# Four transformer layers on one core: another row of the planner's cost table, more of the MLP's blocks evacuated by VectorE, and a new order list

## The chip, the cores and the metric

The kernel runs on one core of a Trainium2 chip. The metric is the device time of one execution in microseconds (us). Three runs of the kernel before gave 449.42, 451.48 and 449.11 us, so the median is 449.42 us.

The core has five engines, each with its own instruction stream. TensorE (PE) multiplies matrices into PSUM, a memory of eight banks of 128 x 512 f32. PE's records come in two rows, PEld for the loading of the 128-row stationary operand and PE for the matmul itself. ScalarE (ACT) computes Exp and GELU. VectorE (DVE) and GpSimd (POOL) do the elementwise work, and only DVE and ACT read PSUM here. SyncE (SP) issues most of the DMAs.

## The reference

One sequence of 2048 tokens with 512 features goes through attention, MLP, attention, MLP, each behind a layernorm without gain and added to the residual. Both attention layers share one set of weights, and both MLP layers another.

```python
def _A_ref(x, wqkv, wo):                      # D = 512, H = 32 heads of 16, W = 256
    qkv = (x @ wqkv).reshape(B, S, 3, H, Dh).transpose(2, 0, 3, 1, 4)
    q, k, v = qkv[0], qkv[1], qkv[2]
    scores = einsum("bhqd,bhkd->bhqk", q, k) * Dh ** -0.5
    mask = (i - j >= 0) & (i - j < W)         # each query sees itself and 255 keys before it
    p = softmax(where(mask, scores, -1e9))
    return einsum("bhqk,bhkd->bhqd", p, v).transpose(...).reshape(B, S, D) @ wo

def _B_ref(x, w1, b1, w2, b2):                # F = 1792
    return gelu(x @ w1 + b1, approximate=True) @ w2 + b2

x = x + A(layernorm(x)); x = x + B(layernorm(x))
x = x + A(layernorm(x)); x = x + B(layernorm(x))
```

## The kernel before, in words

**Tiles.** The 2048 tokens are 16 tiles of 128; the two passes over the layers make 32 tiles in a row (`NT`), and two tiles make a block of attention, so there are 16 blocks (`NB`). All weights stay on the core, as does the residual `X`.

**Attention of a block.** Q and K (the Q group at `lnq`, the K group at `kv`) and V are projected from the transposed, normalised tile `xnTA`. The scores come in *visits* of 512 columns (function `visit`). A visit is 16 or 24 short matmuls on a quarter of the array's rows each, four of them side by side, and takes four PSUM banks. Two Exps on ACT (L948), each 128 x 1024, take the visit to `E`. There are 152 visits and 304 Exps. A mask (L969, on DVE or POOL) clears the triangles. Then `pv` multiplies `E` with `Va` in two *halves* of 64 matmuls, each of 17 columns of the array, for every pair of chunks of heads; DVE transposes the result (L1034), divides by the sums (L1037, L1039) and transposes again (L1044); `outproj` multiplies with `Wo`.

**MLP.** The 32 tiles are ten jobs (`JOBS`): two of 2 tiles, six of 4 tiles, two of 2 tiles. A job has 14 blocks of 128 hidden features (`FC`), each of four matmuls over 256 or 512 columns. GELU is taken in one of two ways. For the first `NPRE(J)` blocks DVE adds the bias and copies from PSUM to `gT` (L1103), and ACT then takes GELU of two blocks at once inside `gT` (L1106). For the other blocks ACT reads PSUM itself, with the bias (L1114). The last two jobs, which start when attention has ended, use only the second way. Then 14 matmuls of 512 columns per tile multiply with `W2`, and DVE adds to `X` (L790).

**What sets the order.** All operations are nodes with an engine, a duration and dependencies (`_List.add`). A list of node numbers written out by hand, `ORDER`, sets the order on every engine: each engine does its nodes in the order of the list. `TURNS` says, for each node that two engines could do (masks, PSUM evacuations of Q and V, the division), which one does it. `BANKS` gives the PSUM banks of each group. `_List.run` walks the list with a table of costs to get planned starts, which `_Sched.spread` uses to place some of PE's waits; the order itself comes from `ORDER`. Semaphore waits are worked out from the reads and writes.

**PE's code in the cost table.** One row of the table, `CODE`, says how the planner sees PE's instruction stream: an edge after 194 instructions and then after every 256, 2.009 instructions for each matmul, and a time after each edge before which PE may not go past the next one. In `_List.run`:

```python
                while edge < till:
                    at = nd["start"] + late + nd["dur"] * (edge - code) / (till - code)
                    late += max(0.0, loaded - at)
                    loaded = max(at, loaded) + self.CODE[3]
                    edge += self.CODE[1]
```

The program on PE has 8764 matmuls, each with its load of the stationary operand, and some 80 instructions that only wait: 69 pieces of 256 instructions.

Of the kernel before, what the change touches and what calls it, by code (L numbers as in the profile page):

```python
# [185 lines left out]
class _List:  # L186
# [5 lines left out]
    CODE = (194.0, 256.0, 2.0090, 3700.0)  # L192
# [38 lines left out]
    def run(self):  # L231
# [11 lines left out]
        last_lock = None  # L243
        code, edge, loaded = 2.0, self.CODE[0], 0.0
        last_geo, last_tab = None, "exp"
# [53 lines left out]
def bass_interleave_layers__sliding_block__dense_activation_gelu__prompt_kernel(  # L299
# [60 lines left out]
    def NPRE(J):  # L360
        return 10 if J < 2 else 6
# [13 lines left out]
    with ExitStack() as kctx:  # L375
        S_ = _Sched(nc, kctx)

        def sb(name, shape, dtype=dt.bfloat16):
# [832 lines left out]
```

## Time and profile before

| | |
|---|---|
| median of three runs | 449.42 us (449.11 to 451.48) |
| the profiled execution's own time | 449.14 us |
| its span, first to last instruction | 447.4 us |
| granted TensorE clock | 1.000 |
| PE busy | 425.2 us, 95% |
| PEld busy | 232.2 us, 52% |
| DVE busy | 373.5 us, 83% |
| ACT busy | 386.4 us, 86% |
| POOL busy | 239.9 us, 54% |

The profiled execution ran 449.14 us, 1.74 us of which lie outside the span. A busy PE in this table is not a PE at its peak, because a matmul's record covers the array's latency also, and the records of successive matmuls overlap: for the pace the reader should take the starts of successive matmuls. PEld rows are the more exact ones for where PE stood still, because each matmul has one load just ahead of it. "issue" as the releaser of a wait means that no semaphore event of the profile ended it.

### The profile page before, as it was taken

Reading aid. Unit: us, or ns where it says so; the run is one execution under the profiler, and the core shown is the slowest. Engines: PE = TensorE matmul, PEld = TensorE weight load, DVE = VectorE, ACT = ScalarE, POOL = GpSimd, SP = SyncE. Lnnn points to the kernel's source line nnn. Section 1 sums busy time; section 2 is a strip of 40 time slices with the busy share of each in tenths; the row PEclk is TensorE's granted clock in tenths of the full one; section 3 lists DMA queues with packets and bytes.
Section 4 is the critical chain, followed back from the end, with each engine's and each line's share of the span. In section 5 each row is a group of like instructions: output and inputs, shape, how many; then the busy total and the mean of one; then the engine's idle time right before and its main releaser. Section 6 shows DMA issues by size and latency. Waiting matters only on the chain.

```text
span 447.4 us, 19245 instructions
## 1 busy us (share of the span) xinstructions
PE 425.2 (95%) x8691; PEld 232.2 (52%) x8764; DVE 373.5 (83%) x745; ACT 386.4 (86%) x458; POOL 239.9 (54%) x301
## 2 busy tenths in 40 slices
PE   8999999888999999999999999999999999999997
PEld 5555655645544545545445445445454454545665
DVE  6999989899998989888999898998898876775512
ACT  2999999999999998899997999889979999892452
POOL 4764786755865357643356457672455454444330
DMA  9920000001120112010220101301031003002021
GB/s 264 370 88 4 4 1 3 5 3 50 43 56 13 50 51 75 25 37 16 68 67 3 39 24 50 74 15 49 27 85 50 15 5 94 22 8 62 0 84 48
DMA packets 39903, 22.88 MB, mean 51 GB/s; under 512 B 24460, under 2 KB 39308, under 8 KB 39820
## 3 DMA queue, kind: packets, MB, share of 16 engines
q1 hardware_dynamic: 39404, 21.24, 16.4%
q8 instruction: 69, 1.13, 1.0%
q10 hardware_dynamic: 416, 0.39, 0.3%
q14 instruction: 14, 0.11, 0.1%
HBM read 13.77 MB, written 7.86 MB: 48 GB/s over the span
## 4 chain that ended last, share of the span: by engine, by line
PE 70%; ACT 15%; DVE 10%; issue 2%; DMA 2%; POOL 0%
PE ps L32 69%; ACT E L948 10%; ACT gT L1114 2%; ACT gT L1106 2%; DVE TT L1034 2%; DVE E L969 1%; DMA xnTB<-scr_x 1%; DVE stat L734 1%; DVE QT L720 1%; ACT L948 1%; DVE X L790 1%; DVE xs_ L753 1%; DMA scr_x<-xs_ 1%; DVE Va L720 1%; DVE OT L1044 1%
## 5 line engine op out<-in xcount | busy, mean ns | idle before, releaser
L948 ACT ACTIVATE E<-ps 128x1024 bf16<-128x1024 f32 x304 | 285.7, 1044 | 23.9 <-PE ps L32 23.0
L969 POOL TENSOR_TENSOR E<-E,mask 128x512 bf16<-128x512 bf16 (+1 forms) x130 | 134.8, 1052 | 89.9 <-DVE E L969 40.8
L32 PE MATMUL ps<-xnTB,W_sb 128*128 128x512 bf16 (+1 forms) x560 | 115.2, 337 | 1.4 <-issue 0.3
L32 PE MATMUL ps<-W_sb,gT 128*128 128x512 bf16 (+1 forms) x421 | 108.4, 373 | 4.3 <-issue 3.0
L32 PE MATMUL ps<-xnTA,Wqkv_sb 128*128 128x256 bf16 (+1 forms) x544 | 74.6, 267 | 1.5 <-ACT E L948 0.7
L32 PEld LDWEIGHTS ps<-xnTB,W_sb 128*128 128x128 bf16 x560 | 51.6, 98 | 42.9 <-ACT E L948 3.8
L32 PE MATMUL ps<-QT,KT 32*64 32x320 bf16 (+4 forms) x2976 | 65.5, 258 | 4.0 <-ACT E L948 2.0
L790 DVE TENSOR_TENSOR X<-X,ps 128x512 bf16<-128x512 bf16 x63 | 42.4, 676 | 25.3 <-PE ps L32 25.0
L32 PEld LDWEIGHTS ps<-W_sb,gT 128*128 128x128 bf16 x462 | 41.5, 98 | 42.2 <-issue 6.7
L1114 ACT ACTIVATE gT<-ps,b1T 128x512 bf16<-128x512 f32 (+1 forms) x84 | 45.7, 598 | 20.1 <-PE ps L32 19.8
L32 PEld LDWEIGHTS ps<-xnTA,Wqkv_sb 128*128 128x128 bf16 x544 | 47.0, 98 | 24.2 <-ACT E L948 3.5
L32 PEld LDWEIGHTS ps<-QT,KT 32*64 32x64 bf16 x2976 | 27.6, 103 | 51.0 <-ACT E L948 32.5
L969 DVE TENSOR_TENSOR E<-E,mask 128x512 bf16<-128x512 bf16 (+1 forms) x132 | 49.1, 402 | 3.0 <-ACT E L948 3.0
L741 POOL TENSOR_TENSOR statmv<-statmv,mhalf 128x1 f32<-128x1 f32 x64 | 36.6, 575 | 22.8 <-DVE statmv L738 18.9
L32 PE MATMUL ps<-E,Va 64*17 64x128 bf16 (+3 forms) x3872 | 46.0, 229 | 2.5 <-ACT E L948 0.9
L1034 DVE STREAM_TRANSPOSE TT<-ps 128x1024 f32<-128x1024 f32 x32 | 39.8, 1244 | 9.4 <-PE ps L32 9.1
L32 PEld LDWEIGHTS ps<-E,Va 64*17 64x17 bf16 x3872 | 36.7, 85 | 19.5 <-PE ps L32 8.0
L1039 POOL TENSOR_TENSOR TM<-TT,Rc 128x512 bf16<-128x512 f32 x22 | 23.3, 1058 | 44.0 <-DVE E L969 17.8
L734 DVE BATCH_NORM_STATS2 stat<-X 128x6 f32<-128x512 bf16 x64 | 43.0, 678 | 2.7 <-DMA X<-in_A_x_dram 2.4
L1078 POOL TENSOR_TENSOR X<-X,b2b 128x512 bf16<-128x512 bf16 x32 | 36.7, 1157 | 13.2 <-DVE E L969 5.7
L1103 DVE TENSOR_SCALAR gT<-ps,b1T 128x512 bf16<-128x512 f32 (+1 forms) x56 | 35.5, 643 | 8.0 <-PE ps L32 7.7
L864 DVE TENSOR_TENSOR KT<-ps,parmask 128x1024 bf16<-128x1024 f32 x30 | 36.2, 1210 | 2.7 <-PE ps L32 2.5
(56 smaller groups left out, 348.5 us busy)
## 6 DMA issues: line engine op xcount, KB each, us to landing
scr_x<-xs_ SPq DMA_DIRECT2D x44, 128.0 KB, 1.9
W_sb<-in_B_w_dram SPq DMA_DIRECT2D x2, 1792.0 KB, 15.4
xnTB<-scr_x SPq DMA_DIRECT2D x26, 128.0 KB, 2.7
xnTA<-scr_x SPq DMA_DIRECT2D x18, 128.0 KB, 2.7
out_dram<-X SPq DMA_DIRECT2D x15, 128.0 KB, 1.8
Wqkv_sb<-in_A_wqkv_dram SPq DMA_DIRECT2D x4, 256.0 KB, 4.9
X<-in_A_x_dram SPq DMA_DIRECT2D x1, 1024.0 KB, 9.2
Wqkv_sb<-in_A_wqkv_dram SPq DMA_DIRECT2D x1, 512.0 KB, 6.4
```

Of the source, the lines that this page charges most:

```text
L32: return self.e.matmul(*a, **k)
L734: add("dve", lambda e, B: e.bn_stats(stat6[:, k6, :], X[:, t, :]), 590, reads=["X%d" % t], writes=["st%d" % k6], prio=prio)
L741: add("pool", lambda e, B: e.tensor_tensor(out=statmv[:, k, 1:2], in0=statmv[:, k, 1:2], in1=mhalf[:], op=ALU.pow), 535, reads=["ve%d" % k ...
L790: add("dve", lambda e, B: e.tensor_tensor(out=X[:, t, :], in0=X[:, t, :], in1=ps[:, B[g][0], :], op=ALU.add), d_psum(512), reads=["X%d" % ...
L864: add("dve", lambda e, B, g=g, i=i: e.tensor_tensor(out=KT[:, kb, :, 2 * i : 2 * i + 2, :].rearrange("p a c q -> p a (c q)"), in0=ps[:, B[ ...
L948: add("act", lambda e, B, g_=g_, gi=gi: e.activation(E[:, 2 * gi : 2 * gi + 2, e0 : e0 + 512], ps[:, B[g_][0] : B[g_][0] + 2, :], AF.Exp, ...
L969: op = lambda e, B, Ew=Ew, Mw=Mw: e.tensor_tensor(out=Ew, in0=Ew, in1=Mw, op=ALU.mult)
L1034: add("dve", lambda e, B: e.transpose(TT[:, s].rearrange("p a c q d -> p a (c q d)"), ps[:, B[g][0] : B[g][0] + 2, :].rearrange("p a n -> ...
L1039: mul = lambda e, B: e.tensor_tensor(out=TM[:, sm].rearrange("p c q a d -> p a (c q) d"), in0=TT[:, s, :, :, :, 0:Dh].rearrange("p a c q d ...
L1078: add("pool", lambda e, B: e.tensor_tensor(out=X[:, t, :], in0=X[:, t, :], in1=b2b[:], op=ALU.add), 1110, reads=["X%d" % t, "b2b"], writes ...
L1103: add("dve", lambda e, B, g=g, fc=fc: e.tensor_scalar(out=gT[:, fc, 0:M], in0=ps[:, B[g][0], 0:M], scalar1=b1T[:, fc : fc + 1], scalar2=No ...
L1114: add("act", lambda e, B, g=g, fc=fc: e.activation(gT[:, fc, 0:M], ps[:, B[g][0], 0:M], AF.Gelu_apprx_tanh, bias=b1T[:, fc : fc + 1], scal ...
```

## The change

Three things are edited. The fourth number of `CODE` goes from 3700 to 3000 (ns). `NPRE` goes from 10 and 6 to 12 and 8, so that in the first two jobs 12 of 14 blocks, and in the next six 8 of 14, are evacuated by VectorE ahead of a GELU inside SBUF. `ORDER`, `TURNS` and `BANKS` are replaced as a whole. The number in `CODE` puts no instruction into the program; it enters the planned starts, which decide where some of PE's waits are placed.

```diff
-    CODE = (194.0, 256.0, 2.0090, 3700.0)
+    CODE = (194.0, 256.0, 2.0090, 3000.0)
...
     def NPRE(J):
-        return 10 if J < 2 else 6
+        return 12 if J < 2 else 8
...
         ORDER = [
-            18, 21, 22, 23, 24, 25, 26, 27, 28, 29, 15, 16, 4, 5, 0, 8, 9, 10, 3, 17, 1, 2, 14, 35, 19, 36, 37, 38,
...
+            3222, 3228, 3229, 3230, 3231, 3232, 3233, 3234, 3235, 3236, 3237, 3238,
         ]
         TURNS = [
-            1, 1, 0, 1, 1, 1, 1, 1, 0, 0, 0, 0, 1, 0, 1, 0, 1, 0, 1, 0, 0, 0, 0, 0, 1, 1, 1, 0, 1, 1, 0, 0, 1, 1, 1,
...
+            1, 1, 0, 1, 1, 0, 0, 1, 0, 1, 0, 0, 1, 1, 1, 0, 1, 0, 1, 0, 0, 0, 0, 0, 1, 1, 0, 1, 1, 0, 1, 1, 1, 1, 0,
...
         BANKS = (
-            "2 6 0 7 5 4 2 6 3 1 6 5 0 1267 3467 5 2 0134 7 6 4523 1 2367 0 5 3412 0 7 5 1267 0 6734 5 2 0134 67 "
...
+            "2 6 1 0 7 3 5 6 2 0 6 7 1234 0 5634 7 2 0134 7 6 4523 6 4501 7 2 3 0167 3 5 6745 1 2367 0 1 4523 67 "
```

Counted in the two programs, these instructions change their number; everything else, PE's 8764 matmuls, the 304 Exps, the 18 table loads of ACT and all DMAs included, is there as often as before, in another order:

| engine, operation, output | before | after |
|---|---|---|
| DVE bias and copy to `gT`, 128x512 / 128x256 | 36 / 20 | 48 / 24 |
| ACT GELU from PSUM, 128x512 / 128x256 | 48 / 36 | 36 / 32 |
| ACT GELU inside `gT`, 128x1024 / 128x512 | 18 / 10 | 24 / 12 |
| evacuation of V, 128x512: DVE / ACT | 25 / 7 | 18 / 14 |
| evacuation of Q, 128x512: DVE / ACT | 29 / 5 | 28 / 6 |
| evacuation of Q, 128x256: DVE / ACT | 0 / 4 | 2 / 2 |
| evacuation of `xnTA`: DVE / ACT | 12 / 2 | 11 / 3 |
| evacuation of `xnTB`: DVE / ACT | 4 / 2 | 5 / 1 |
| mask 128x512: DVE / POOL | 116 / 102 | 111 / 107 |
| division of the attention output: DVE / POOL | 10 / 22 | 8 / 24 |
| epsilon of the layernorm: DVE / POOL | 29 / 35 | 25 / 39 |

414 rows, old and new, of tables (BANKS, ORDER, TURNS) are left out of this document.

## The prediction

> **What bounds the kernel now.** I read the page first (busy shares, the chain), then three stretches, then who waits on PE's side.
>
> ```profile
> span 447.4 us, 19245 instructions
> PE 425.2 (95%) x8691; PEld 232.2 (52%) x8764; DVE 373.5 (83%) x745; ACT 386.4 (86%) x458; POOL 239.9 (54%) x301
> PE 70%; ACT 15%; DVE 10%; issue 2%; DMA 2%; POOL 0%
> ```
> ```profile
> core 0: us, PE busy (x) PEld busy (x) DVE busy (x) ACT busy (x) POOL busy (x), PEclk, DMA share, GB/s
> 20.00:120.00 100.00, 91.03 (x2318) 54.30 (x2330) 92.88 (x198) 97.75 (x115) 67.72 (x76) 1.00 0.09 27
> 120.00:400.00 280.00, 272.26 (x5653) 139.37 (x5700) 245.98 (x471) 258.11 (x291) 146.56 (x175) 1.00 0.16 42
> 400.00:447.40 47.40, 44.10 (x520) 27.92 (x522) 18.96 (x39) 19.13 (x39) 14.37 (x19) 1.00 0.15 46
> ```
>
> Two stages have two bounds. From 20 to 120 us ACT is busy 97.75 of 100 us: Exp sets the pace. From 120 to 400 PE is busy 272.26 of 280 while ACT and DVE have 22 and 34 us to spare, and after 400 PE runs alone. A microsecond that PE stands still between 120 and 447 is lost unless another of its waits shrinks for it. Over PE's waits from 120 to 400 (total us, times, longest):
>
> ```profile
> PEld ps L32 <- ACT E L948: 32.0, 89, 0.6
> PEld ps L32 <- issue: 16.3, 72, 0.4
> ...
> PEld ps L32 <- ACT gT L1114: 2.1, 6, 0.5
> PEld ps L32 <- DVE gT L1103: 1.9, 5, 0.4
> ...
> PEld ps L32 <- DMA xnTB<-scr_x: 0.8, 1, 0.8
> ```
>
> Most of this passes while the matmul before still runs, but the list says whom PE meets: Exp, 89 times.
>
> **Code edges, the part the change speaks of.** PE's code comes in by DMA, in 69 packets, so 16 KB or some 254 instructions each (twice 8764 over 69). The row below is the page's; the next two rows are the DMA rates of 79 to 83 us in slices of 0.1 us, where no other transfer runs, and of 27 to 29 us in slices of 0.05; then PE's loads around two stands.
>
> ```profile
> q8 instruction: 69, 1.13, 1.0%
> ```
> ```profile
> GB/s 0 0 164 0 0 0 0 0 0 0 0 0 0 0 0 0 0 0 0 0 0 0 0 0 0 0 0 0 0 0 0 0 0 0 0 0 0 164 0 0
> ```
> ```profile
> GB/s 0 0 0 0 0 0 0 0 0 0 0 0 0 0 0 0 0 0 0 0 0 0 0 0 0 0 0 0 0 0 0 0 0 328 0 0 0 0 0 0
> ```
> ```profile
> 26.83 0.15 PEld L32 LDWEIGHTS ps<-QT,KT 32*64 32x64 bf16 x15 [0.21 <-DVE QT L720]
> 27.57 0.10 PEld L32 LDWEIGHTS ps<-QT,KT 32*64 32x64 bf16 x1 [0.58 <-issue]
> ```
> ```profile
> 80.92 0.40 PEld L32 LDWEIGHTS ps<-E,Va 64*17 64x17 bf16 x29
> 81.68 0.12 PEld L32 LDWEIGHTS ps<-E,Va 64*17 64x17 bf16 x11 [0.36 <-issue]
> ```
> ```profile
> 0.00:27.56 27.56, 24.87 (x344) 14.88 (x348) 23.24 (x52) 18.98 (x24) 17.05 (x40) 1.00 0.91 292
> 0.00:81.67 81.67, 74.21 (x1610) 43.76 (x1619) 73.36 (x163) 71.83 (x86) 53.00 (x81) 1.00 0.31 101
> ```
>
> PE stands in the middle of a visit for 0.58 us and in the middle of a PV half for 0.36, and no semaphore ends it. Where: 348 loads lie ahead of the first, 1619 ahead of the second; with as many matmuls and the program's 7 and 25 wait instructions that is 703 and 3263, and both are 191 more than a multiple of 256. So these are code edges. A packet starts at 79.2 to 79.3, PE goes over the edge at 81.68, 2.4 us later; the next packet starts at 82.7 to 82.8, 1.1 us after the crossing, as at the other place (27.57, packet at 28.65). So PE seems unable to cross two edges less than 2.4 + 1.1 = 3.5 us apart. I count with 3.55.
>
> **The price of the new edges.** I add up PE's own pace between successive edges (instructions 192 + 256k) in both programs' orders. The pace, from starts of successive instructions:
>
> ```profile
> 413.36 2.75 PE L32 MATMUL ps<-W_sb,gT 128*128 128x512 bf16 x12 [0.16 <-issue]
> 416.82 1.91 PE L32 MATMUL ps<-xnTB,W_sb 128*128 128x256 bf16 x16
> ```
> ```profile
> 207.40 0.21 PEld L32 LDWEIGHTS ps<-QT,KT 32*64 32x64 bf16 x24 [0.42 <-ACT E L948]
> 207.76 0.10 PEld L32 LDWEIGHTS ps<-W_sb,gT 128*128 128x128 bf16 x1
> ```
> ```profile
> 412.45 0.61 PEld L32 LDWEIGHTS ps<-E,Va 64*17 64x17 bf16 x64 [0.42 <-PE ps L32]
> 413.12 2.49 PEld L32 LDWEIGHTS ps<-W_sb,gT 128*128 128x128 bf16 x13
> ...
> 413.32 1.25 DVE L1034 STREAM_TRANSPOSE TT<-ps 128x1024 f32<-128x1024 f32 x1 [0.32 <-PE ps L32]
> ```
>
> A 512-column matmul takes (2.75-0.38)/11 = 0.216 us, a 256-column one 0.109, a visit 0.36, a PV half 0.67 (0.38 and 0.27 being single records). One block as an example, the 30th: before it holds 1.03 PV halves, 1.84 visits, 4 long and 12 short matmuls, 3.5 us; after it holds 1.5 halves, one visit, 1 long and 6 short ones, 2.2 us.
>
> In PE's stage, 120 us on, before has six blocks under 3.55 us (3.33, 3.10, 3.39, 3.45, 3.53, 3.54), 1.0 us short together. The new order has eleven (3.32, 3.10, 2.99, 2.84, 2.18, 3.23, 3.37, 3.11, 3.50, 3.44, 2.54), 5.4 us short. In ACT's stage there are six before (5.1 us short) and five after (3.30, 2.29, 2.43, 1.78, 2.12; 5.8 us short).
>
> What is paid of the 5.4: waits inside a block lengthen it. PE met Exp for 32.0 of 280 us, 0.34 us per 3 us block; taken off each short, at most all of it, leaves 2.5. If the close blocks hold no waits it is 5.4. I take 3.6, nearer 2.5, because each stand also lets ACT and DVE run ahead and a later wait shrinks. Before pays a part of its 1.0 too: at the edge in the row below 0.27 us are idle where some 0.12 lie between two such loads (0.216 less the load's 0.10), so 0.15; over the six I take 0.35.
>
> ```profile
> 172.05 0.53 PEld L32 LDWEIGHTS ps<-W_sb,gT 128*128 128x128 bf16 x3 [0.27 <-issue]
> ```
>
> So **+3.2 us**, between +2.1 and +5.1 if the floor of 3.5 holds.
>
> [...]
>
> **Semaphore waits in the new order.** For every wait of PE on ACT, DVE or POOL I take PE's pace between the matmul that feeds the other engine and the waiting one, and set against it the durations on the path (Exp below) with 0.34 us for two hops, an estimate from the 0.26 us between the end of the PV loads (413.06) and the transpose (413.32). Where the pace is shorter, PE comes too early. Those shortfalls sum to 27.2 us before and 24.8 after; beyond the first 100 us of PE's work, 6.2 and 5.7. In PE's stage that is **-0.4**. In ACT's stage PE's earliness costs nothing as long as ACT runs on: I take 0 there, with -2.0 (the rest of the difference) and +2.0 (edges starving ACT) as ends.
>
> **VectorE ahead of GELU, and the moved evacuations.** By form:
>
> ```profile
> L948 ACT ACTIVATE E<-ps 128x1024 bf16<-128x1024 f32 x304 | 285.7, 1044 | 23.9 <-PE ps L32 23.0
> ...
> L1114 ACT ACTIVATE gT<-ps,b1T 128x512 bf16<-128x512 f32 x48 | 30.0, 692 | 1.7 <-PE ps L32 1.7
> ...
> L1103 DVE TENSOR_SCALAR gT<-ps,b1T 128x512 bf16<-128x512 f32 x36 | 26.6, 740 | 6.7 <-PE ps L32 6.4
> ...
> L1106 ACT ACTIVATE gT<-gT 128x1024 bf16<-128x1024 bf16 x18 | 18.7, 1056 | 0.0
> ...
> L720 DVE CAST Va<-ps 128x512 bf16<-128x512 f32 x25 | 16.9, 680 | 1.8 <-PE ps L32 1.7
> ...
> L1114 ACT ACTIVATE gT<-ps,b1T 128x256 bf16<-128x256 f32 x36 | 15.7, 472 | 18.4 <-PE ps L32 18.1
> ...
> L1103 DVE TENSOR_SCALAR gT<-ps,b1T 128x256 bf16<-128x256 f32 x20 | 9.0, 469 | 1.4 <-PE ps L32 1.3
> ...
> L1106 ACT ACTIVATE gT<-gT 128x512 bf16<-128x512 bf16 x10 | 6.0, 626 | 0.0
> L722 ACT ACTIVATE Va<-ps 128x512 bf16<-128x512 f32 x7 | 4.3, 611 | 0.0
> ```
>
> ACT loses 12 x 692 + 4 x 472 = 10.2 us and gains 6 x 1056 + 2 x 626 = 7.6; seven evacuations of V come to it, 7 x 611 = 4.3; the other moves cancel to -0.2. ACT: +1.5 us. DVE gains 12 x 740 + 4 x 469 = 10.8, loses 7 x 680 = 4.8 and some 4 of masks and small operations: +2.0. POOL has half its time idle. In PE's stage ACT's 22 and DVE's 34 spare us cover this; without that cover ACT's share would add 1.1. In ACT's stage nothing covers it: ACT's work ahead of the 57th visit (some 120 us) grows by 0.4 by the same sums: **+0.4**. PSUM banks come free sooner when DVE takes a block: at most the 2.1 us of PE's waits on L1114; but 1.9 us of waits on L1103 stand beside it and grow with the count (72 against 56). I take 0.
>
> **SP and the table.** Each of the 44 round trips through DRAM, all in other places of SP's queue, has the same two DMAs; one late arrival was met by PE, 0.8 us, so -0.8 to +0.8, taken 0. The 18 table loads of ACT stay.
>
> **The sum.** +3.2 - 0.4 + 0.4 = +3.2 us on a span of 447.4: 450.6, and with the 1.74 us outside the span 452.3 us. The profiled execution (449.14) lies 0.28 below the median of 449.42; against the median it is +0.6%.
>
> **The rivals.** *The stands are hidden anyway* (no change): PE pauses at an edge, ACT and DVE catch up, and the next wait on Exp is shorter. For it: 32.0 us of such waits, 89 of them. Against it: the largest shorts (1.37, 1.01, 0.71 us) are longer than any wait there (0.6). It gives some +1, 450 us. *The edges are free below 3.5 us* (faster): the two stands were something else, a block that is asked for sooner comes sooner, and the new order keeps its better waits: -2.4 of shortfalls, -0.35 of stands, 446.4 us. It decides if PE goes over edges 3 us or less apart without an idle record there; nothing in this trace tries that without a stand. [...] *The edges starve ACT* (slower still): two blocks of 1.78 and 2.12 us lie in ACT's stage; a stand of 1.8 us in front of a visit is longer than one Exp (1.04), so ACT runs dry: another +2 to +3, 455 us. *The change doesn't do what it says*, the new order's edges being spread by waits anyway, falls together with the first rival.
>
> **How the numbers follow.** Forecast 0.48 (450.6 to 455), hidden 0.25, free 0.17, starving 0.10. Half a percent, 2.25 us, is what a measurement of this kernel tells from no change: below 447.2 lies the "free" case, 0.17; "hidden" and the low end of the forecast give 0.31 within; the rest, 0.52, is slower. The range runs from 447.0 to 456.0: down to a partly free edge, up to starving with the full 5.1.
>
> **What would show it.** Right: idle records of PEld with "issue" as releaser, 0.3 to 1.4 us, inside visits and PV halves at multiples of 256 (plus 191) instructions; no two code packets less than 3.5 us apart; PE's total wait on Exp a little lower. Wrong: packets 3 us apart or less without stands (free); stands there but the wait on Exp shrinking by the same (hidden); ACT's busy share in 20 to 120 us falling under 97 (starving).

## The result, and the profile after

The changed kernel takes 451.31 us (median of 20 runs), the kernel before 449.69 us (20 runs beside it): a ratio of 1.0035, 95% interval 1.0024 to 1.0046. So the change costs 1.6 us. The profiled execution of the changed kernel ran 450.97 us; its span and its busy engines are these, from the head of its page and from the chain of work that ended last:

```profile
span 449.1 us, 19322 instructions
...
PE 433.7 (97%) x8764; PEld 232.7 (52%) x8764; DVE 379.2 (84%) x744; ACT 388.1 (86%) x456; POOL 248.5 (55%) x312
...
PE 77%; ACT 18%; DMA 1%; DVE 1%; issue 1%; SPq 1%
```

The same three stretches as before, with the same columns:

```profile
core 0: us, PE busy (x) PEld busy (x) DVE busy (x) ACT busy (x) POOL busy (x), PEclk, DMA share, GB/s
20.00:120.00 100.00, 92.27 (x2303) 53.86 (x2308) 92.94 (x198) 97.64 (x113) 72.24 (x81) 1.00 0.09 28
120.00:400.00 280.00, 277.41 (x5723) 139.61 (x5706) 247.16 (x465) 258.00 (x290) 153.48 (x184) 1.00 0.16 41
400.00:449.10 49.10, 46.30 (x533) 28.61 (x530) 23.38 (x44) 20.35 (x40) 12.53 (x16) 1.00 0.15 47
```

ACT is as busy as before in its own stage (97.64 against 97.75 us) and in PE's stage (258.00 against 258.11). The busy time of the PE row rose by 5 us from 120 to 400, but that row counts overlapping records and had more of them missing before (5653 records against 5723); the waits of PEld say more. First before, from 20 to 120 us (its rows from 120 to 400 stand in the prediction); then after, from 20 to 120; then after, from 120 to 400. The columns are total us, times, and longest.

```profile
PEld ps L32 <- ACT E L948: 13.3, 37, 0.8
PEld ps L32 <- issue: 5.0, 22, 0.6
```

```profile
PEld ps L32 <- ACT E L946: 15.6, 43, 0.8
PEld ps L32 <- issue: 7.8, 31, 0.9
```

```profile
PEld ps L32 <- ACT E L946: 29.6, 83, 0.8
PEld ps L32 <- issue: 18.0, 73, 1.5
```

Two things moved in opposite directions. Waits that no semaphore ended ("issue") grew, by 2.8 us in ACT's stage and 1.7 us in PE's, and the longest went from 0.4 to 1.5 us in PE's stage. All waits on other engines and on DMAs together (the whole list but PE's waits for itself added up) shrank, from 24.6 to 22.5 us in ACT's stage and from 44.8 to 40.7 us in PE's.

The long "issue" waits lie where the prediction said, at multiples of 256 (plus 191) instructions. From the loads of the changed kernel, edge 15 in ACT's stage and edges 28, 30 and 41 in PE's:

```profile
98.10 0.42 PEld L32 LDWEIGHTS ps<-xnTA,Wqkv_sb 128*128 128x128 bf16 x4 [0.79 <-issue]
...
173.12 0.31 PEld L32 LDWEIGHTS ps<-Wqkv_sb,xv 128*128 128x128 bf16 x2 [0.60 <-issue]
...
180.96 0.26 PEld L32 LDWEIGHTS ps<-QT,KT 32*64 32x64 bf16 x24
182.76 0.55 PEld L32 LDWEIGHTS ps<-Wqkv_sb,xv 128*128 128x128 bf16 x4 [1.53 <-issue]
...
258.14 0.10 PEld L32 LDWEIGHTS ps<-W_sb,gT 128*128 128x128 bf16 x1 [0.59 <-DVE Rc L1035]
```

At 182.76 (edge 30) PE stands for 1.5 us with four matmuls of a V projection ready to go. At edge 41 (258.14) the profile names a semaphore wait on DVE. The count that this load waits for was reached at 257.59 us, with the end of DVE's transpose, 0.55 us before the load; so some 0.4 of the 0.59 us may be the edge's too. The table leaves them out. I call the excess of such a gap over the gap that the same pair of loads has elsewhere in the two traces a *stand*. Added up over the edges, the stands are (a gap of 0.27 us in before at edge 1, whose code had come 4.1 us earlier, is not counted):

| | before | after |
|---|---|---|
| ACT's stage (to 120 us) | 1.5 us | 3.1 us (edges 6, 11, 12, 15, 17: 0.53, 0.58, 0.27, 0.78, 0.88) |
| PE's stage (from 120 us) | 0.36 us | 2.5 us (edges 26, 28, 30, 44, 48: 0.38, 0.48, 1.36, 0.11, 0.18) |
| all | 1.8 us | 5.6 us |
| span less stands | 445.6 us | 443.5 us |

So the stands grew by 3.8 us and the kernel by 1.7 us of span: if a stand is lost at its full length, everything else in the change must have gained about 2 us. Where each came is told by how far Exp has got. The busy time of the Exp line alone, up to a point near 123 us, before and then after:

```profile
0.00:123.20 123.20, 96.47 (x104) 1.00 0.24 76
```

```profile
0.00:123.40 123.40, 96.50 (x103) 1.00 0.24 75
```

At the end of ACT's stage the changed kernel is some 0.2 us late, although its stands there are 1.6 us more; the other 1.5 us of its loss come after that, where its stands are 2.1 us more. On the same condition that leaves a gain of 1.4 us for the rest of the change in ACT's stage, and of 0.6 us in PE's. Two questions follow, and the experiments are made for them: is a stand really lost time, in both stages, and is the gain of the rest real?

### The profile page after: what moved, and what is told of

It is laid out like the page before. It is cut to its first block, busy times and chain, and to the rows that moved or that the text cites. A ratio compares the mean times of both kernels' runs of the same rounds, so it can differ in the third digit from the quotient of the medians.

```text
span 449.1 us, 19322 instructions
## 1 busy us (share of the span) xinstructions
PE 433.7 (97%) x8764; PEld 232.7 (52%) x8764; DVE 379.2 (84%) x744; ACT 388.1 (86%) x456; POOL 248.5 (55%) x312
## 3 DMA queue, kind: packets, MB, share of 16 engines
q8 instruction: 69, 1.13, 1.1%
## 4 chain that ended last, share of the span: by engine, by line
PE 77%; ACT 18%; DMA 1%; DVE 1%; issue 1%; SPq 1%
PE ps L32 77%; ACT E L946 13%; ACT gT L1104 2%; DMA Wqkv_sb<-in_A_wqkv_dram 1%; ACT gT L1112 1%; ACT L946 1%; ACT L1104 1%; PE ps L36 1%; SPq L696 0%; DVE stat L732 0%; DVE gT L1101 0%; DVE TT L1032 0%; DVE Va L718 0%; ACT Va L720 0%; ACT QT L720 0%
## 5 line engine op out<-in xcount | busy, mean ns | idle before, releaser
L967 POOL TENSOR_TENSOR E<-E,mask 128x512 bf16<-128x512 bf16 (+1 forms) x135 | 140.4, 1056 | 80.8 <-DVE E L967 38.5
L32 PE MATMUL ps<-W_sb,gT 128*128 128x512 bf16 (+1 forms) x462 | 117.8, 374 | 0.1
L32 PE MATMUL ps<-xnTB,W_sb 128*128 128x512 bf16 (+1 forms) x560 | 112.9, 337 | 0.2
L967 DVE TENSOR_TENSOR E<-E,mask 128x512 bf16<-128x512 bf16 (+1 forms) x127 | 53.0, 442 | 5.8 <-ACT E L946 5.3
L1101 DVE TENSOR_SCALAR gT<-ps,b1T 128x512 bf16<-128x512 f32 (+1 forms) x72 | 46.1, 652 | 10.0 <-PE ps L32 9.5
L1112 ACT ACTIVATE gT<-ps,b1T 128x512 bf16<-128x512 f32 (+1 forms) x68 | 35.6, 584 | 21.6 <-PE ps L32 21.4
L1037 POOL TENSOR_TENSOR TM<-TT,Rc 128x512 bf16<-128x512 f32 x24 | 25.4, 1056 | 22.5 <-DVE E L967 11.5
```

What stands on the lines that cost most here:

```text
L32: return self.e.matmul(*a, **k)
L967: op = lambda e, B, Ew=Ew, Mw=Mw: e.tensor_tensor(out=Ew, in0=Ew, in1=Mw, op=ALU.mult)
L1037: mul = lambda e, B: e.tensor_tensor(out=TM[:, sm].rearrange("p c q a d -> p a (c q) d"), in0=TT[:, s, :, :, :, 0:Dh].rearrange("p a c q d ...
L1101: add("dve", lambda e, B, g=g, fc=fc: e.tensor_scalar(out=gT[:, fc, 0:M], in0=ps[:, B[g][0], 0:M], scalar1=b1T[:, fc : fc + 1], scalar2=No ...
L1112: add("act", lambda e, B, g=g, fc=fc: e.activation(gT[:, fc, 0:M], ps[:, B[g][0], 0:M], AF.Gelu_apprx_tanh, bias=b1T[:, fc : fc + 1], scal ...
```

## The experiments

All ratios are to the kernel before, in runs on the same chip, with their 95% interval.

### The order of before, with nothing moved but its edges

The kernel before runs 8 and then 5 matmuls on zeros on PE before any data is there. Cutting the five into 13 or 35 of nearly the same total of columns (2548 and 2555 in place of 2560) moves every later edge by 16 or 60 instructions against the matmuls, and moves nothing else.

```diff
-        def clear(n):
+        def clear(n, w):
...
-                    r = e.matmul(ps[:, b, :], gT[:, 0, 0:P], zero, start=True, stop=True)
+                    r = e.matmul(ps[:, b % 8, 0:w], gT[:, 0, 0:P], zero[:, 0:w], start=True, stop=True)
...
-        for n, took in ((8, 3420.0), (5, 1500.0)):
+        for n, w, took in ((8, 512, 3420.0), (13, 196, 1500.0)):
```

> The kernel before in its own order, with the five last matmuls that warm PE up before any data is there cut into thirteen of the same total of columns. Nothing else moves but every edge, 16 instructions earlier in the program. What the blocks lack of 3.55 us, waits inside them taken off, goes from 0.5 to 5.9 us in PE's stage (edges 26, 28, 30, 32, 41 at 1.0 to 1.5 us each) and from 1.3 to 3.3 in ACT's. Theory (paid): +2 to +4.5 us, 452 to 454. Rival (hidden): less than +0.7. Rival (edges free): 0.

> The same with 35 in place of the five matmuls, edges 60 instructions earlier: the lack goes from 0.5 to 15.0 us in PE's stage and from 1.3 to 8.5 in ACT's, in stands of 1.1 to 2.0 us each. Theory (paid): +8 to +14 us from PE's stage, and none to +5 from ACT's if ACT starves there: 458 to 468. Rival (hidden): less than +2. Rival (edges free): 0.

Measured: 455.0 us with 13 (1.0126, 1.0111 to 1.0140) and 466.58 us with 35 (1.0384, 1.0351 to 1.0417). Eight more matmuls at a place where PE has nothing to do cost 5.4 us, thirty cost 17. The same loads around edge 41, in before and then with 13:

```profile
253.70 0.64 PEld L32 LDWEIGHTS ps<-E,Va 64*17 64x17 bf16 x68 [0.20 <-issue]
254.38 0.98 PEld L32 LDWEIGHTS ps<-W_sb,gT 128*128 128x128 bf16 x6
```

```profile
257.85 0.64 PEld L32 LDWEIGHTS ps<-E,Va 64*17 64x17 bf16 x68 [0.20 <-issue]
259.74 0.98 PEld L32 LDWEIGHTS ps<-W_sb,gT 128*128 128x128 bf16 x6 [1.25 <-issue]
```

The second kernel is 4.15 us late ahead of the edge and 5.36 us behind it. As the order is the same, this subtraction can be made for every one of the 8764 loads, and the curve of lateness is a staircase: nearly flat between edges, with a step at an edge (one step of 0.4 us, near 225 us, comes at a semaphore wait). With 13 matmuls it goes from -0.2 us at 20 us to 1.9 at 120 us (lasting steps of 0.4, 0.2, 0.2, 0.7 and 0.5 at edges 2, 11, 12, 15 and 17; at edge 15 a stand of 1.2 us, of which the next wait gave 0.5 back), to 3.8 behind edges 26 and 28, to 5.2 behind edge 41, and stays at 5.1 to the end. Only one lasting step was given back whole, 0.5 us at edge 46, by a later wait. With 35 it is 7.2 us at 120 us and 19.6 at the end, but not all of this is stands: behind three of them (edges 6, 15 and 46) the granted clock fell (to 0.57, 0.71 and 0.61 on average of the 4 us from 48, 104 and 300 us), and 1.25, 1.1 and 1.0 us more were lost there (see the last section). Its six runs lie between 463.99 and 468.96 us, with mean clocks from 1.000 to 0.989; the fastest, at full clock, is still 14 us above before. This decides three points:

- The stands are not hidden. PE's wait on Exp from 120 to 400 us hardly shrank (31.7 us with 13, against 32.0), while "issue" rose from 16.3 to 19.1:

```profile
PEld ps L32 <- ACT E L948: 31.7, 88, 0.6
PEld ps L32 <- issue: 19.1, 72, 1.3
```

- The edges are not free: the same matmuls in the same order take 1.3% and 3.8% longer when only the edges lie elsewhere.
- Stands are paid in ACT's stage as in PE's: 2.1 of the 5.4 us fall before 120 us, and with 35 matmuls 7.6 of the 20 us (2.4 of them through the clock), although ACT is the busier engine there. My expectation for the first run, made from PE's stage alone, was too low for this reason; the second run lies within its range.

### The order of after, its close blocks widened by moving work

Fifteen groups of matmuls (projections and MLP blocks, with what hangs on them) go from ahead of a PV pair to between its halves, so that the blocks at edges 26, 28, 30, 41 and 48 last 3.7 us or more. A second kernel treats edges 6 and 11 also. Around edge 48, for example, one MLP matmul node and its evacuation (2185, 2186) move behind a visit (the rows are shown with other line breaks):

```diff
         ORDER = [
...
-            2185, 2326, 1932, 2186, 2144, 2161, 2116, 2155, 2157, 2327, 2145,
+            2326, 1932, 2144, 2161, 2116, 2155, 2157, 2327, 2185, 2186, 2145,
```

> The kernel after, with only the close edges of PE's stage widened: 15 groups of matmuls and what hangs on them (Q, K and V projections and MLP blocks) move from ahead of a PV pair to between its two halves, so that the blocks that end at edges 26, 28, 30, 41 and 48 go from 3.14, 2.94, 2.27, 3.30 and 3.23 us of PE's own pace to 3.73 or more; edge 65's block goes from 2.59 to 2.76 only. All else is as in the kernel after. Theory (a stand at an edge is paid): in the profile of after the stands at edges 26 to 48 sum to 2.0 us and should vanish, so 1.4 to 2.0 us faster than after, near 449.6. Rival (stands are hidden, the 1.6 us come from elsewhere in the new order): within 0.5 us of after, 451.3.

> The same, and also the blocks ending at edges 6 and 11, in ACT's stage, widened from 2.43 and 2.51 to 3.81 and 3.70 us (eleven more groups moved); the two blocks at edges 15 and 17 stay (1.82 and 2.15 us). Theory of the prediction (in ACT's stage PE's stands cost nothing while ACT has work): within 0.3 us of the run with PE's stage alone. Rival (the edges starve ACT): the two stands were 0.53 and 0.58 us, so up to 1.1 us faster than that run.

Measured: 457.76 us (1.0194, 1.0179 to 1.0210) and 461.42 us (1.0262, 1.0244 to 1.0280). Both are far slower than the kernel after, against every expectation. The stands did go: "issue" from 120 to 400 us is 15.0 us in the first of the two, 3.0 less than after. Its waits on other things rose by more (from the list of waits in that stretch, and one row of its loads):

```profile
PEld ps L32 <- issue: 15.0, 69, 0.4
...
PEld ps L32 <- ACT gT L1112: 5.0, 6, 3.4
PEld ps L32 <- DVE X L788: 3.0, 6, 1.3
```

```profile
261.54 0.10 PEld L32 LDWEIGHTS ps<-Wo_sb,OT 128*128 128x128 bf16 x1 [3.38 <-ACT gT L1112]
```

After had 1.1 and 1.2 us of these two. The move at edge 41 made two MLP blocks late, their GELUs came behind an Exp in ACT's queue (257.88 us), and PE waited 3.4 us for one PSUM bank. Each change between Exp and GELU also has a table load of 1.28 us on ACT: there are 20 of them in these two kernels, against 18 in before and after, and the two more lie in this place. These runs show what a place in the order is worth, more than a stand; as a test of the stands they failed.

### The order of after, its edges moved by waits that are already satisfied

To open the close blocks without moving work, instructions can be added where blocks are long. A wait on a count that was reached long ago is one instruction more in the program (162 of them and 64 halved matmuls, 290 instructions, take the order of after from 69 code packets to 70 further down). Up to four were put ahead of a long matmul, 256 in all, which shifts the later edges.

```diff
+    PADS = (
+        (613, 1), (614, 1), (615, 1),
...
+        (1159, 4), (1162, 4), (1163, 4),
...
+    )
...
+        for x, c in self.PADS:
+            taken[x] = [("dve", 1)] * (2 * c)
         for x, ws in taken.items():
```

> The kernel after with 256 extra wait instructions on PE, on a count of DVE that has long been reached, one to six of them ahead of each of some 126 projection and MLP matmuls of 256 or 512 columns. They move no work; they shift the later edges against the matmuls, by 22 instructions from the 5th block, up to 240 by the 19th and 256 at the end, so that the close blocks become longer. Reading the trace of after with its stands taken out and the edges at their new places, 0.3 us is left to stand at edge 6, 0.3 at 27 and at most 0.8 at 66 (its counterpart in after, 65, had no stand). Theory (stands are paid whole, in both stages): 5.1 us of stands become 0.6 to 1.4, so 3.7 to 4.5 us faster than after less what 256 satisfied waits cost; at 0 to 5 ns each, 0 to 1.3: 446.8 to 449. Rival (only the stands of PE's stage are paid): 1.5 to 2 us faster, 449.5. Rival (the order itself costs the 1.6 us, not its edges): no faster than 450.5.

> The same with all 256 placed in PE's stage, from the 22nd block on, so that the stands at edges 26, 30 and 48 (2.0 us in the profile of after) go and those of ACT's stage (3.0 us at edges 6 to 17) stay. Theory: 1.5 to 2.0 us faster than after less the cost of the waits: 449.3 to 450.5.

> The same with all 256 between the 5th and the 20th block, so that the stands of ACT's stage become 0.3 us while those of PE's stage fall one edge later, at 27, 29, 31 and 49, and stay. Theory (stands are paid in ACT's stage too): 2.0 to 2.8 us faster than after less the cost of the waits: 448.5 to 449.8. Prediction's term (stands there cost nothing while ACT has work): within 0.5 us of after, 451.3.

> The kernel before with 256 such waits at places where no new close block comes up and its own (0.2 to 0.4 us each, at edges 6, 11, 12, 15, 17) open. It prices the waits: its own stands to be gained are 0.4 to 1.0 us, so 448.6 to 449.2 if a satisfied wait costs nothing, 449.9 to 450.5 if it costs 5 ns.

Measured: 456.91 (1.0162, 1.0134 to 1.0190), 458.24 (1.0170, 1.0132 to 1.0208), 458.16 (1.0194, 1.0172 to 1.0215) and, for the kernel before, 460.55 us (1.0250, 1.0228 to 1.0273). All of them slow, and the last says why: it is 11 us slower, and by its staircase against before some 9.4 us of that fall where its 256 satisfied waits stand, 0.04 us each and not 0 to 5 ns, an expectation for which no trace had a figure. Much of the rest are new stands (1.25 us at edge 15 the longest). Its loads where four such waits stand ahead of each matmul:

```profile
73.77 0.10 PEld L32 LDWEIGHTS ps<-W_sb,gT 128*128 128x128 bf16 x1 [0.35 <-DVE statmv L755]
74.21 0.10 PEld L32 LDWEIGHTS ps<-W_sb,gT 128*128 128x128 bf16 x1 [0.35 <-DVE E L986]
```

These loads follow at 0.44 us, where the prediction worked out 0.216 us for such matmuls. By the same staircase, the price sits where two or more waits share a matmul: 44 at 22 matmuls cost 2.3 us and 68 at 17 cost 3.5, while 10 at 10 and 6 at 6 cost 0.0. Ahead of 256-column matmuls in a row, one added 0.02 us at most and two 0.12. One satisfied wait ahead of a long matmul is free, a second is not. So the three runs of after can't be read by their times. One thing can be read from the first against after (its profiled execution ran 454.37 us, the fastest of its five): behind the last of its waits in ACT's stage (121 us) it is 5.0 us late, and by 190 us only 3.6, since the stands of after at edges 26, 28 and 30 (0.38, 0.48, 1.36) are no longer there. About 1.0 us of this is lost again behind the last, at 187.21 us, and not to an edge: the matmul there waits for a DMA of `xnTB`, whose last packet landed at 187.10, 1.9 us after the others.

### The same without a price

Now 54 of the 512-column matmuls in the middle of a sum become two of 256 columns (one matmul more, the same columns), and no matmul gets more than one satisfied wait.

```diff
+        if halve:
+            out, w, x = a
+            n = x.shape[1] // 2
+            self.e.matmul(out[:, 0:256], w, x[:, 0:n], **k, skip_group_check=True)
+            return self.e.matmul(out[:, 256:512], w, x[:, n:], **k, skip_group_check=True)
...
+        for x in self.WAIT2:
+            taken[x] = [("dve", 1)] * 2
```

> The kernel after with its edges moved by 256 instructions in all that should cost nothing this time: 54 projection and MLP matmuls of 512 columns become two of 256 columns each, and 148 matmuls of 256 or 512 columns get one satisfied wait each (in the run with up to six at one matmul, one at one matmul cost 0, two or more some 0.1 us). By the trace of after with its stands taken out, 0.3 us is left to stand at edge 6, 0.3 at 27, and at most 0.8 at 66. Theory (stands are paid in both stages; the rest of the change is a gain): 5.1 us of stands become 0.6 to 1.6, so 3.5 to 4.5 us faster than after, less 0 to 1 for the added instructions: 446.8 to 448.8. Rival (only PE's stage pays): 449.3 to 450. Rival (the new order itself costs the 1.6 us): 450.5 or more.

> The kernel before treated in the same way (55 halved, 146 waits), so that its own close edges open too: 1.7 us of stands, of which those at edges 6 to 19 (0.8 us) can go, less 0 to 1 for the added instructions: 448.6 to 449.8. Set beside the kernel after in the same treatment it shows what the rest of the change is worth with the edges out of the way: theory, 1 to 2.5 us for the order of after; rival, nothing or less.

Measured: 450.27 us (1.0028, 1.0014 to 1.0041) for the order of after and 450.07 us (1.0027, 1.0012 to 1.0042) for the order of before. The additions are indeed free: in the staircases, a block with 16 halved matmuls and 20 waits (order of after, behind edge 8) and one with 38 waits (order of before, behind edge 6) are within 0.1 us of their old length. But the order of after gained 0.5 us only. Its trace shows old stands gone and new ones come, two of them in blocks that should have been long enough:

```profile
73.76 0.17 PEld L38 LDWEIGHTS ps<-E,Va 64*17 64x17 bf16 x24 [0.28 <-PE ps L38]
75.48 0.47 PEld L38 LDWEIGHTS ps<-E,Va 64*17 64x17 bf16 x40 [1.55 <-issue]
...
325.90 0.14 PEld L38 LDWEIGHTS ps<-E,Va 64*17 64x17 bf16 x17 [0.23 <-PE ps L38]
328.08 0.51 PEld L38 LDWEIGHTS ps<-E,Va 64*17 64x17 bf16 x47 [2.04 <-issue]
```

PE had crossed the edges before these at 70.3 and 322.1 us. The DMA rates from 69.5 to 74 us, in 40 slices, show when the code for the first of them came:

```profile
GB/s 0 0 0 0 0 0 0 0 0 0 0 0 0 0 0 0 0 0 0 0 0 0 0 0 0 0 0 0 0 0 0 146 0 0 0 0 0 0 0 0
...
q8 instruction: 1, 0.02, 1.4%
```

The packet starts in the 32nd slice, at 73.0 to 73.1 us, 2.8 us after the crossing and not 1.0 to 1.1, and nothing else was on the DMA queues. The other came 3.6 us after its crossing. So a block of 3.55 us is not safe; some packets come late. My expectation for this run (3.5 us and more to gain) fell, and the two treated orders, at the same time, seemed to say that the rest of the change gains nothing. But they stood for about 6.0 and 2.8 us in their profiled executions: their spans less stands are 443.6 and 445.2 us, 1.6 us apart, where those of after and before are 2.1 apart. (The profiled execution of the first ran 451.37 us, 1.1 above its median.)

### Once more, with room to spare

The places are chosen again, now so that as many blocks as can be are longer than needed (64 halved, 162 waits; the edit is as above with other numbers).

> The kernel after treated once more (64 matmuls of 512 columns halved, 162 single waits, 290 instructions in all), with the places chosen so that as many blocks as possible keep some spare time beyond 3.55 us, because in the treated run before it two code packets came 2.5 and 3.6 us after the crossing of an edge instead of 1.0, and cost 1.6 and 2.1 us in blocks that were only just long enough. By the traces of after and of that run, the blocks at edges 6, 27, 11 and 13 are left at 3.06, 3.24, 3.63 and 3.55 us, all others at 3.58 or more. Theory (the stands of after are paid and the rest of the change is a gain of 1.5 to 2 us): below the kernel before, 447.3 to 449.0. Rival (the rest of the change gains nothing): 449.5 to 450.5, as the two treated kernels so far.

Measured: 448.60 us (12 runs), ratio 0.9983 (0.9971 to 0.9995). It is 2.3 us faster than the kernel after by the two ratios (1.0035 less 0.9983 is 0.52% of 449.3 us), and 0.17% faster than the kernel before, so that it beats both, the latter by little. From its page, and its waits from 120 to 400 us:

```profile
span 447.1 us, 19536 instructions
```

```profile
PEld ps L38 <- ACT E L975: 30.6, 85, 0.8
PEld ps L38 <- issue: 15.4, 68, 0.6
```

"Issue" is down from 18.0 to 15.4 us, and the wait on Exp is 1.0 us longer than in after and still 1.4 shorter than in before. The place of after's longest stand (180.96 and 182.76 above) now reads:

```profile
179.68 0.27 PEld L38 LDWEIGHTS ps<-QT,KT 32*64 32x64 bf16 x24
180.03 0.55 PEld L38 LDWEIGHTS ps<-Wqkv_sb,xv 128*128 128x128 bf16 x4
```

This kernel is 1.28 us ahead of after in front of that place and 2.73 us behind it. Its staircase against after goes down by the size of after's stands where after had stood at edges 11, 12, 15, 17, 26, 28 and 30, and part of that comes back at the next waits: what lasts is 0.35, 0.14, 0.58, 0.65, 0.38, 0.48 and 1.13 us of stands of 0.58, 0.27, 0.78, 0.88, 0.38, 0.48 and 1.36. That is 1.7 of 2.5 us in ACT's stage and 2.0 of 2.2 in PE's, where the one part that came back (0.3 us behind edge 30) went to a DMA of `xnTB` that landed at 181.08 us. The staircase goes up where this kernel stands itself (0.9, 0.9 and 0.6 at edges 2, 6 and 47); it ends at -2.0. About 3.2 us of stands are left in it; the span less stands is 443.9 us, like after's 443.5. So the loss of the change is its edges, and what is left of the change when they are out of the way is a gain: the order of after with 3.2 us of stands is as long (447.1 us of span) as the order of before with 1.8 (447.4). The gain is somewhat under the 2 us reckoned above, since stands in ACT's stage came back to two thirds only. How fast the order of before would be with its places chosen with the same care was not run.

### The second edit alone

`NPRE` at 12 and 8 in the order of before: the direct GELUs of the two blocks concerned become a DVE copy each, where the fourth matmul stood, and one GELU where the later of the two stood.

```diff
     def NPRE(J):
-        return 10 if J < 2 else 6
+        return 12 if J < 2 else 8
```

> The kernel before with the second edit alone: 12 and 8 blocks of the MLP evacuated by DVE ahead of GELU, in the order, banks and turns of before (of the blocks that change, DVE copies where the fourth matmul stood, and one GELU for two stands where the second of theirs did). ACT gets 16 direct evacuations less (10.2 us) and 8 GELUs inside SBUF more (7.6 us), DVE 16 copies more (10.8 us). The prediction's terms: 0 in PE's stage, and ACT's stage 0 to 0.5 us shorter, so 449.0 to 449.7. Rival (the waits on DVE and on the later GELU are met by PE): 450.5 or more.

Measured: 461.66 us (1.0273, 1.0242 to 1.0305). PE's waits over the whole run, which in before were 3.0 us on DVE's copies and 0.4 on the GELU inside SBUF, are now:

```profile
PEld ps L32 <- DVE gT L1101: 7.5, 11, 1.7
PEld ps L32 <- ACT gT L1104: 4.1, 2, 3.7
```

These two rows are 8.2 us longer, of the 10.5 us that the profiled execution (459.65 us, full clock) takes more; four of the six runs, those above 461 us, had a mean clock of 0.992 to 0.996. Stands are 2.0 us here, against 1.8 in before, so edges have no part in it. PE waits for the pair's GELU, which now starts when the second block is copied, and for the copies themselves. I had priced this edit at 0 because DVE and ACT have time to spare. They have, but the order decides whether a matmul is in front of them. The run doesn't say what the edit is worth in an order made for it; it can't be told from the order in after.

## Why the prediction was right, and where its terms were wrong

The forecast was 452.3 us and +2.9 against the median of before; measured were 451.31 and +1.6. That is 0.36%, within the half percent that the prediction counted as no change (chance 0.31), and the time alone lies almost as near to the 450 of "hidden" as to the forecast; what tells them apart is the shifted orders. The mechanism was right: PE stands at edges that come close behind one another (in PE's stage of after its crossings lay 3.27 to 3.93 us apart where it stood), the new order has more such pairs, and at most of the closest PE stands. Step by step:

- *"So PE seems unable to cross two edges less than 2.4 + 1.1 = 3.5 us apart."* Nearly, and in part by luck. The closest packets are 3.34 us apart in after, and PE goes over an edge where it stood 2.2 to 2.7 us after the packet's start (3.0 once), as the prediction read. But neither of the two stands that it took this from lies in a close block: PE had crossed the edge before at 19.74 us for the first and at 76.32 for the second, 7.8 and 5.4 us earlier, and the packets started 5.3 and 2.95 us after these crossings (25.07 and 79.27). These stands were due to late packets; close blocks with a stand were there in before too (edges 6 and 28, 0.21 and 0.15 us). It is no fixed figure: where PE stood in PE's stage of after, its crossings lay 3.27 to 3.93 us apart; at edge 12 it was 4.95, behind a packet that started 2.6 us after the crossing.
- *The price of the new edges, +3.2 (3.6 taken of 5.4, less 0.35).* This is the mis-sized term: in PE's stage the stands are 2.5 us less 0.36, so +2.1 (2.5 with the 0.4 that may belong to edge 41). The 0.35 for before was right, and the lower end of the range (2.5 left after taking the waits off) was the value. That the total fits is partly luck, because 0.34 us of waits taken off every short did not hold edge by edge: by it edges 28, 30 and 65 (0.71, 1.37 and 1.01 short) should have stood 0.37, 1.03 and 0.67 us, and they stood 0.48, 1.36 and 0. Edge 65 in after:

```profile
405.38 1.92 PEld L32 LDWEIGHTS ps<-E,Va 64*17 64x17 bf16 x192 [0.42 <-POOL statmv L739]
407.38 1.62 PEld L32 LDWEIGHTS ps<-W_sb,gT 128*128 128x128 bf16 x9
```

Three PV halves run through in 1.92 us, the edge among them at 406.51, and the next matmuls follow at once. The load at the edge before it lies in a row of 512-column matmuls at 403.56, and the code packet for it starts at 403.41, 0.15 us before that load and not 1.0 behind it. In before, too, the packets at edges 13 and 64, both in a row of MLP matmuls, start 0.9 and 0.8 us before the load (86.40 against 87.28, 400.40 against 401.20). So the packets there come earlier than the loads would have it; why, no run here shows.
- *"In ACT's stage PE's earliness costs nothing as long as ACT runs on: I take 0 there."* Wrong as a mechanism, and right as a number by two errors that cancel. Stands in that stage are paid, as the shifted orders show (2.1 us there with 13 matmuls), which is up to +1.6 us for after; and the semaphore waits that the order saves there count too, which I had as the end of -2.0 and not as the value: -1.4 us with the +0.4 of ACT's work in it. Together +0.2 by the progress of Exp, where +0.4 was forecast. If only two thirds of these stands are lost, as the last run of the order of after has it, both numbers are some 0.5 us smaller.
- *Semaphore waits in PE's stage, -0.4.* About -0.6, by difference of span and stands, if these are lost whole.
- *VectorE ahead of GELU, PSUM banks, SP: 0.* Not told apart inside after, and no run has the new row of the cost table alone. PE's waits on L1112 and L1101 from 120 to 400 us fell (1.1 us on L1112 against 2.1 on L1114 before). Alone, in an order not made for it, the second edit costs 12 us.

Of the rivals, "hidden" and "free" fall with the shifted orders. "The edges starve ACT" was half right: ACT's stage pays its stands, but they were 0.3 to 0.9 us each, not the 1.4 to 1.8 us by which its two closest blocks are short, and ACT's busy share stayed at 97.6. Of the signs that were named, the idle records with "issue" (0.28 to 1.53 us at edges 6, 11, 15, 17, 26, 28 and 30) were there. PE's total wait on Exp fell in PE's stage from 32.0 to 29.6 us, by more than the stands there grew (2.1); that is also the sign which the prediction had named for "hidden", so after's trace alone could not refute that rival. In the shifted order, with nothing else moved, the wait fell by 0.3 us only. The sign that no packets lie closer than 3.5 us missed by 0.16 us.

## What to carry to other kernels

Where an instruction stream is loaded in blocks while the engine runs, as PE's is here (69 packets of 16 KB), where the block edges fall is part of the schedule: eight matmuls added at an idle place cost this kernel 5.4 us, and halving 64 matmuls, with 162 single waits added, gained 2.3. Look for idle records that no semaphore ends, count instructions up to them, and take such a stand at its full length until a trace of the same order, shifted, shows how much is given back (here up to a third of it in ACT's stage). To price a change of phase, lay the old trace and the new one side by side by instruction and read the staircase; moving work to cure a stand can cost more than the stand.

## What the runs showed of the hardware that was not expected

- A code packet usually starts 0.8 to 1.4 us after PE crosses an edge, but some start 2.1 to 3.6 us after it, one with no other transfer running (73.0 us in the first treated order). The one behind edge 11 is late in before, after and the order with 13 matmuls alike (2.95, 2.6 and 2.6 us). The cause is open. Late packets may be why after's runs spread from 449.58 to 453.55 us, before's beside them from 448.74 to 451.48; no trace of these runs shows it.
- One satisfied wait ahead of a 256- or 512-column matmul costs 0.02 us at most; two cost 0.12 us at a 256-column matmul, and four made the spacing of 512-column ones 0.44 us in place of 0.216. Two halves of a 512-column matmul take as long as the whole (0.109 us each against 0.216; a block with 16 halved ones and 20 waits kept its length within 0.1 us).
- Stands near 2 us can cost more than themselves, through the granted clock. With 35 matmuls on zeros, the loads behind edge 46, and then two stretches with the column PEclk third from last:

```profile
299.77 0.14 PEld L32 LDWEIGHTS ps<-QT,KT 32*64 32x64 bf16 x10 [2.06 <-issue]
```

```profile
296.00:300.00 4.00, 2.00 (x129) 1.29 (x113) 3.12 (x5) 2.00 (x3) 2.66 (x5) 1.00 0.42 100
300.00:304.00 4.00, 3.84 (x45) 1.56 (x36) 2.19 (x4) 2.93 (x4) 2.25 (x3) 0.61 0.28 74
```

After this stand the clock was 0.61 on average of 4 us, and the kernel lost another 1.0 us on its staircase. The trace has three such drops, behind edges 6, 15 and 46, and they are of one size: over the 8 us from 45.8, 100 and 300 us the mean clock was 0.785, 0.79 and 0.785 (each from two stretches of 4 us). In the 4 us from 44, 98 and 296 us, at a clock of 1.00, PE was busy for 1.85, 1.80 and 2.00 us. Neither that nor the length of a stand decides alone: around the stand of 2.04 us at 328.08 in the first treated order PE was busy for 1.92 us from 324 to 328, and the clock was 1.00 from 324 to 336. In the order widened at PE's stage alone PE stood for 3.38 us ahead of 261.54, and the mean clock from 120 to 400 us was 1.00. What sets off a drop, these runs don't show.
